# The half-empty low pass of the k, v and q products, written as two 64-row matmuls

## The chip, the cores and the metric

The kernel runs on one core of one Trainium2 chip. The time is device microseconds from launch to end of one execution; three executions of the kernel before took 755.6, 756.94 and 759.04 us, median 756.94. Beside the times there is one profiled execution with its trace.

## The reference

Two layers of linear attention alternate with two layers of a mixture of tiny experts, on x of 2048 x 576 in float32:

```python
def _A_ref(x, wqkv, wo):
    qkv = (x @ wqkv).reshape(B, S, 3, H, Dh)...      # 32 heads of 18
    phi = lambda t: jnp.where(t > 0, t + 1, jnp.exp(t)) + 1e-6
    pq, pk = phi(q), phi(k)
    kv = jnp.einsum("bhsd,bhse->bhde", pk, v)
    num = jnp.einsum("bhqd,bhde->bhqe", pq, kv)
    den = jnp.einsum("bhqd,bhd->bhq", pq, z)[..., None] + 1e-6
    return (num / den).reshape(B, S, D) @ wo
...
x = x + _A_ref(_layernorm(x, axis=-1), A_wqkv, A_wo)
x = x + _B_ref(_layernorm(x, axis=-1), B_w_q, B_k1, B_k2, B_u, B_v)
x = x + _A_ref(_layernorm(x, axis=-1), A_wqkv, A_wo)
x = x + _B_ref(_layernorm(x, axis=-1), B_w_q, B_k1, B_k2, B_u, B_v)
```

The change is in `x @ wqkv`, the products k, v and q of both attention layers.

## The kernel before

The 2048 tokens are 16 tiles of 128. For each tile and layer, `front_T` transposes the normalised x on TensorE (tile ptf) and splits the result in two: a high part, rounded by ScalarE to the matmul's number format (thif, line 102), and the low part that is left (tlof, by VectorE, line 103). The weights are split in the same way into whi and wlo. A product is then high x high + high x low + low x high, summed in PSUM.

The contraction runs over 576 rows, which are four blocks of 128 and one of 64 (block `rem`, number 2). So that block 2 fills the array too, its 64 rows stand twice in the transposed x, and its weights hold the high part in partitions 0 to 63 and the low part in 64 to 127 (`split_mixed`, lines 107 and 108). One pass over block 2 of thif then does high x high and high x low at once. The pass of tlof over block 2 does low x high in its upper 64 rows, and in its lower 64 rows low x low, which the other blocks leave out.

`passes` lists the 14 passes of a product: five of thif with whi, four of thif with wlo, five of tlof with whi. `product` (line 212) issues each pass as two matmuls, one for each part of the 576 columns, which go to two PSUM banks: 288 + 288 for k and q, 252 + 324 for v. That is 28 matmuls a product, and 96 products (16 tiles, two layers, k, v and q). Their results are ppk, ppv and ppq.

The order on each engine is that in which the code is written: `in_order` ties the instructions of TensorE, ScalarE, VectorE and GpSimd, stretch by stretch, to the order in which they were issued. That order is set by loops for the first tiles, by `step2` in the middle, and by long lists of pieces given to `play` in the other stretches. A DMA queue on SyncE brings weights and tiles in.

Other things on TensorE that the text speaks of: the `fold` matmuls (line 550) have 32 columns of stationary operand, and four of them go to four strips of 32 PSUM partitions; kva (lines 283 and 285) sums the attention state; ptf, ptb and pto are transposes (line 197). po (line 517) is the experts' output.

Of the kernel before, what the change touches and what calls it, by code (L numbers as in the profile page):

```python
# [12 lines left out]
F32R = mybir.dt.float32r  # L13
BF16 = mybir.dt.bfloat16
I32 = mybir.dt.int32
AF = mybir.ActivationFunctionType
# [5 lines left out]
S, D, H, DH = 2048, 576, 32, 18  # L22
P = 128
NT = S // P
DK, E, NE = 128, 8, 64
HC = 7 * DH
HALF = D // 2
# [11 lines left out]
def blocks(rem):  # L39

    rows, at = [], 0
    for b in range(NB):
        rows.append((at, b - (b > rem)))
        at += 64 if b == rem else P
    return rows


def passes(rem):
    rest = [b for b in range(NB) if b != rem]
    return ([("hi", b, "hi") for b in range(NB)] + [("hi", b, "lo") for b in rest]  # L50
            + [("lo", b, "hi") for b in range(NB)])
# [6 lines left out]
def network(ctx, tc, x_in, wqkv, wo, wq_t, k_t, u_t, v2, c_mask, c_mask4, c_ident, c_code, c_code1, c_scale, c_shift, out):  # L58
    nc = tc.nc

    cp = ctx.enter_context(tc.tile_pool(name="cp", bufs=1))
# [4 lines left out]
    def psum(name):  # L66
        return ps.tile([P, 1024], F32, tag="ps", name=name)
# [14 lines left out]

    whi = cp.tile([P, NB, 3 * D], F32R, name="whi")
    wlo = cp.tile([P, 4, 3 * D], F32R, name="wlo")
    ohi = cp.tile([P, NB, D], F32R, name="ohi")
    olo = cp.tile([P, NB, D], F32R, name="olo")
    shi = cp.tile([P, NB, 512], F32R, name="shi")
# [12 lines left out]
    def split(src, hi, lo, eng=nc.vector):  # L100

        nc.scalar.activation(hi, src, AF.Copy)  # L102
        eng.tensor_tensor(lo, src, hi.bitcast(F32), op=ALU.subtract)  # L103

    def split_mixed(src, dst):

        nc.scalar.activation(dst, src, AF.Copy)
        nc.vector.tensor_tensor(dst[64:], src[64:], dst[64:].bitcast(F32), op=ALU.subtract)
# [24 lines left out]
    def split_weight(tiles, c0, hi, lo, rem, which=range(NB), eng=nc.vector):  # L133
        for b in which:
            cols = slice(c0, c0 + D)
            if b != rem:
                split(tiles[b], hi[:, b, cols], lo[:, blocks(rem)[b][1], cols], eng)
            else:
                split_mixed(tiles[b], hi[:, b, cols])

    @contextmanager
    def in_order(*engines):
# [62 lines left out]
    def product(tt, hi, lo, cols, n, cut=HALF, rem=REM, by_block=False):  # L205

        o = psum(f"pp{n}")
        todo = sorted(passes(rem), key=lambda p: p[1]) if by_block else passes(rem)
        for i, (a, b, w) in enumerate(todo):
            wb = hi[:, b] if w == "hi" else lo[:, blocks(rem)[b][1]]  # L210
            for c0, c1, at in ((0, cut, 0), (cut, D, 512)):
                nc.tensor.matmul(o[:, at:at + c1 - c0], tt[a == "lo"][:, b, :], wb[:, cols + c0:cols + c1],  # L212
                                 start=(i == 0), stop=(i == len(todo) - 1))
        return o

    def phi(p, n):
# [7 lines left out]
    tt = {}  # L224
# [9 lines left out]
    def front_k(l, t):  # L234
        k = product(tt["f", l, t], whi, wlo, D, f"k{l}_{t}", by_block=(l == 0 and t == 0))
        yield
        tt["fk", l, t] = phi(k, f"k{l}_{t}")

    def front_v(l, t):
        v = product(tt["f", l, t], whi, wlo, 2 * D, f"v{l}_{t}", cut=2 * HC)  # L240
        yield
        vt = v5[t % 2]
        w = HC + 1
        for c, x in ((0, v[:, :2 * HC]), (2, v[:, 512:512 + 2 * HC])):
            nc.scalar.activation(vt[:, c * w:(c + 2) * w].rearrange("p (c e) -> p c e", c=2)[:, :, :HC],
                                 x.rearrange("p (c e) -> p c e", c=2), AF.Copy)
        yield
        nc.scalar.activation(vt[:, 4 * w:4 * w + 72], v[:, 512 + 2 * HC:512 + 2 * HC + 72], AF.Copy)

    def front_q(l, t):  # L250
        q = product(tt["f", l, t], whi, wlo, 0, f"q{l}_{t}")
        yield
        fq = phi(q, f"q{l}_{t}")
        nc.sync.dma_start(pq_d[l][t], fq)
# [438 lines left out]
    with in_order(*ALL):  # L693
        x0, x1 = xs.pop(("f", 0)), xs.pop(("f", 1))
        warm_up(14)
        rs0 = statistics(x0, "f0_0", soon=True)
        split_weight(wk_in, D, whi, wlo, REM, (0,))
        ys["f", 0, 0] = normalized(x0, rs0, "f0_0")
        split_weight(wk_in, D, whi, wlo, REM, (1, 2))
        run(0, (fT, 0, 1))  # L700
        warm_up(2)
        run(0, (fT, 0))
        split_weight(wk_in, D, whi, wlo, REM, (3,), nc.gpsimd)
        rs1 = statistics(x1, "f0_1", soon=True)
        split_weight(wk_in, D, whi, wlo, REM, (4,))
# [145 lines left out]
```

## Time and profile before

| | |
|---|---|
| median of three executions | 756.94 us |
| span of the profiled execution, first to last instruction | 753.7 us |
| matmuls | 5356 |
| VectorE busy | 456.8 us |
| ScalarE busy | 289.1 us |
| GpSimd busy | 197.7 us |
| DMA moved | 79.48 MB |

The profiled execution's span is the time from its first to its last instruction; the profile gives no further time for it, so what lies around the span is taken from the median, 3.2 us. In the rows, PE is TensorE's matmuls, PEld its weight loads, DVE VectorE, ACT ScalarE, POOL GpSimd. A timeline row gives start and length in us, engine, line, operation, the tile written and the tiles read, and how many instructions the row takes together. Where an engine was idle before, the bracket gives for how long and who released it. Line numbers are those of the kernel before.

### The profile page before, as it was taken

What the parts mean: (1) busy time and instruction counts of PE and PEld (TensorE: products, weight loads), DVE (VectorE), ACT (ScalarE), POOL (GpSimd) and SP (SyncE); (2) the same over time, 40 slices, a digit from 0 to 9 for tenths busy, and PEclk for the clock granted to TensorE, in tenths of its full rate; (3) what the DMA queues carried; (4) which work ended last, traced back from release to release, by engine and by line L of the source; (5) the groups of instructions that cost most, each with busy time, mean ns of one, the idle gap of its engine ahead of it and who ended that gap; (6) DMA issues with size and microseconds to landing.
All of it is one profiled execution on the core that took longest, in us unless ns stands there. A gap on an engine that the chain in (4) does not pass through costs nothing.

```text
span 753.7 us, 13987 instructions
## 1 busy us (share of the span) xinstructions
PE 736.8 (98%) x5356; PEld 693.2 (92%) x5356; DVE 456.8 (61%) x1008; ACT 289.1 (38%) x586; POOL 197.7 (26%) x540
## 2 busy tenths in 40 slices
PE   7999999999999999999999999999999999999996
PEld 5999989999998989999999999999999999999984
DVE  5532342324246887666666665563366789999996
ACT  5422232232333544444444443533234333343443
POOL 2110001000002543333333342230033343534331
PEclk9999999999999999999999999999999999999999
DMA  9736446631111322222232211321733213111201
GB/s 275 245 125 223 157 171 220 218 118 49 48 63 32 110 89 77 98 84 83 92 105 101 83 67 60 111 68 38 206 107 112 85 65 115 48 48 58 70 33 63
DMA packets 52267, 79.48 MB, mean 105 GB/s; under 512 B 5480, under 2 KB 22376, under 8 KB 52200
## 3 DMA queue, kind: packets, MB, share of 16 engines
q1 hardware_dynamic: 52200, 78.59, 31.8%
q8 instruction: 42, 0.69, 0.4%
q14 instruction: 25, 0.20, 0.1%
HBM read 55.01 MB, written 23.56 MB: 104 GB/s over the span
## 4 chain that ended last, share of the span: by engine, by line
PE 81%; DVE 10%; ACT 3%; issue 2%; POOL 2%; DMA 1%; SPq 0%; DVEq 0%; POOLq 0%; ACTq 0%
PE ppk L212 15%; PE ppv L212 15%; PE ppo L402 13%; PE pps L433 12%; PE ppq L212 11%; PE kva L283 4%; PE fold_ps L550 2%; PE ptf L197 2%; PE ptb L197 2%; PE po L517 2%; PE pto L197 2%; PE m L332 1%; DVE tloo L103 1%; DVE o L379 1%; DVE x L391 1%
## 5 line engine op out<-in xcount | busy, mean ns | idle before, releaser
L219 DVE TENSOR_SCALAR ek<-ek 128x576 f32<-128x576 f32 x32 | 14.7, 459 | 81.4 <-ACT ek L218 76.9
L212 PE MATMUL ppk<-whi,thif 128*128 128x288 f32 x320 | 50.4, 301 | 1.6 <-ACT thif L102 1.6
L402 PE MATMUL ppo<-ohi,thio 126*128 126x288 f32 (+1 forms) x320 | 50.9, 301 | 0.8 <-DVE ct L492 0.5
L212 PEld LDWEIGHTS ppk<-whi,thif 128*128 128x128 f32 x320 | 44.2, 188 | 5.6 <-issue 3.3
L163 POOL TENSOR_SCALAR rsf<-mvf 128x1 f32<-128x1 f32 x16 | 3.1, 192 | 175.6 <-DVE mvf L161 175.4
L212 PE MATMUL ppk<-whi,tlof 128*128 128x288 f32 x320 | 48.7, 296 | 0.3 <-DVE tlof L103 0.3
L212 PE MATMUL ppv<-whi,thif 128*128 128x252 f32 x320 | 48.0, 296 | 0.1
L187 ACT ACTIVATE yb<-x,rsb 128x640 f32<-128x640 f32 x32 | 29.5, 923 | 47.9 <-POOL rsb L180 47.9
L212 PE MATMUL ppv<-whi,tlof 128*128 128x252 f32 x320 | 47.6, 295 | 0.0
L219 DVE TENSOR_SCALAR eq<-eq 128x576 f32<-128x576 f32 x32 | 15.8, 493 | 51.7 <-ACT eq L218 51.7
L433 PE MATMUL pps<-shi,thib 128*128 128x512 f32 x160 | 44.4, 407 | 2.0 <-ACT thib L102 2.0
L402 PEld LDWEIGHTS ppo<-ohi,thio 126*128 126x128 f32 (+1 forms) x320 | 44.6, 189 | 1.9 <-issue 0.7
L212 PEld LDWEIGHTS ppk<-whi,tlof 128*128 128x128 f32 x320 | 44.6, 188 | 0.5 <-DVE tlof L103 0.5
L212 PEld LDWEIGHTS ppv<-whi,tlof 128*128 128x128 f32 x320 | 44.6, 188 | 0.0
L212 PEld LDWEIGHTS ppv<-whi,thif 128*128 128x128 f32 x320 | 44.2, 188 | 0.3 <-ACT thif L102 0.3
L438 ACT ACTIVATE s<-pps 128x512 f32<-128x512 f32 x32 | 19.1, 596 | 61.4 <-PE pps L433 61.4
L433 PE MATMUL pps<-shi,tlob 128*128 128x512 f32 x160 | 42.5, 395 | 0.0
L103 DVE TENSOR_TENSOR tlof<-ptf,thif 128x640 fp32r<-128x640 f32 x32 | 26.2, 818 | 24.3 <-ACT thif L102 24.2
L402 PE MATMUL ppo<-ohi,tloo 126*128 126x288 f32 x256 | 40.3, 295 | 0.0
L402 PE MATMUL ppo<-olo,thio 126*128 126x288 f32 x256 | 40.3, 296 | 0.0
L212 PE MATMUL ppk<-wlo,thif 128*128 128x288 f32 x256 | 39.9, 296 | 0.0
L212 PE MATMUL ppq<-whi 128*128 128x288 f32 x260 | 39.6, 299 | 0.1
(156 smaller groups left out, 1778.6 us busy)
## 6 DMA issues: line engine op xcount, KB each, us to landing
fold<-in_wq_t SPq DMA_DIRECT2D x64, 288.0 KB, 4.8
whi<-hl_d SPq DMA_DIRECT2D x26, 320.0 KB, 3.5
pq_d<-eq SPq DMA_DIRECT2D x19, 288.0 KB
pq<-pq_d SPq DMA_DIRECT2D x19, 288.0 KB, 3.3
xf<-in_x SPq DMA_DIRECT2D x16, 288.0 KB, 4.7
x<-in_x SPq DMA_DIRECT2D x16, 288.0 KB, 2.8
x_d<-x SPq DMA_DIRECT2D x16, 288.0 KB, 3.1
x<-x_d SPq DMA_DIRECT2D x16, 288.0 KB, 2.6
```

Source lines behind the costliest of these rows:

```text
L103: eng.tensor_tensor(lo, src, hi.bitcast(F32), op=ALU.subtract)
L187: nc.scalar.activation(y, x2, AF.Identity, scale=rs[:, 0:1], bias=rs[:, 1:2])
L197: nc.tensor.transpose(pt[:, b * P:(b + 1) * P], x, ident)
L212: nc.tensor.matmul(o[:, at:at + c1 - c0], tt[a == "lo"][:, b, :], wb[:, cols + c0:cols + c1], start=(i == 0), stop=(i == len(todo) - 1))
L219: nc.vector.tensor_scalar(e, e, 1.0, EPS, op0=ALU.min, op1=ALU.add)
L283: nc.tensor.matmul(a[:w, c * HC:(c + 1) * HC], vt[:, c * w:(c + 1) * w], fk[:, c * HC:(c + 1) * HC], start=(t == 0 and c == 0), stop=(t == ...
L332: nc.tensor.matmul(m[:c, h * 512:h * 512 + HALF], kvb[:n, b * HC:b * HC + c], wob[l][b][:n, h * HALF:(h + 1) * HALF], start=True, stop=True)
L402: nc.tensor.matmul(p[:, h * 512:h * 512 + HALF], hl[a][:r, b], w[:r, h * HALF:(h + 1) * HALF], start=(i == 0), stop=(i == len(todo) - 1))
L433: nc.tensor.matmul(p[:, :512], hl[a == "lo"][:, b, :], shi[:, b] if w == "hi" else slo[:, blocks(REM)[b][1]], start=(i == 0), stop=(i == l ...
L438: nc.scalar.activation(s[:, NE:], p[:, :512], AF.Copy)
L517: nc.tensor.matmul(p[:, b * 512:b * 512 + HALF], c[i], vmix[:, b * HALF:(b + 1) * HALF], start=(i == 0 and not based), stop=(i == 1))
L550: nc.tensor.matmul(p[32 * j:32 * j + 32, at:at + c1 - c0], kpad[:, ch // 2, 24 - 8 * a:56 - 8 * a], st[:, c0:c1], start=(a == 0), stop=(a ...
```

## The change

The pass of tlof over block 2 is taken out of the list of passes and written as two matmuls of 64 rows. The first takes rows 0 to 63 of the array (tlof's upper copy of the block with whi) for the first part of the columns. The second takes rows 64 to 127 (tlof's lower copy) for the other part of the columns, into the other PSUM bank. For the second one the high weights are needed in partitions 64 to 127, where whi holds low parts: they are put into a new tile wx, by one more ScalarE copy for each of k, v and q. What was low x low in that pass is no longer computed.

The pair stands last in k and q, and first in v. In the very first product of k, whose passes go block by block, the pair moves from the middle to the end.

```diff
+    wx = cp.tile([P, 2 * HALF + D - 2 * HC], F32R, name="wx")
...
             else:
+                cut, at = upper(c0)
+                nc.scalar.activation(wx[64:, at:at + D - cut], tiles[b][64:, cut:], AF.Copy)
                 split_mixed(tiles[b], hi[:, b, cols])
+
+    def upper(c0):
+
+        return {0: (HALF, 0), D: (HALF, HALF), 2 * D: (2 * HC, 2 * HALF)}[c0]
...
         todo = sorted(passes(rem), key=lambda p: p[1]) if by_block else passes(rem)
-        for i, (a, b, w) in enumerate(todo):
+        todo.remove(("lo", rem, "hi"))
+        todo = [None] + todo if cols == 2 * D else todo + [None]
+        for i, p in enumerate(todo):
+            flags = dict(start=(i == 0), stop=(i == len(todo) - 1))
+            if p is None:
+                at = upper(cols)[1]
+                nc.tensor.matmul(o[:, :cut], tt[1][:64, rem, :], hi[:64, rem, cols:cols + cut], **flags)
+                nc.tensor.matmul(o[:, 512:512 + D - cut], tt[1][64:, rem, :], wx[64:, at:at + D - cut], **flags)
+                continue
+            a, b, w = p
             wb = hi[:, b] if w == "hi" else lo[:, blocks(rem)[b][1]]
             for c0, c1, at in ((0, cut, 0), (cut, D, 512)):
-                nc.tensor.matmul(o[:, at:at + c1 - c0], tt[a == "lo"][:, b, :], wb[:, cols + c0:cols + c1],
-                                 start=(i == 0), stop=(i == len(todo) - 1))
+                nc.tensor.matmul(o[:, at:at + c1 - c0], tt[a == "lo"][:, b, :], wb[:, cols + c0:cols + c1], **flags)
```

The order on the engines, at three places. First TensorE at the border of k and v of tile 2, layer 0. A row gives the line, the operation, the tile written, the tiles read, partitions x columns of the output, and how many in a row. Before:

```order
L212 MATMUL ppk_2_556<-whi,thif_2_447 128x288 x10
L212 MATMUL ppk_2_556<-wlo,thif_2_447 128x288 x8
L212 MATMUL ppk_2_556<-whi,tlof_2_448 128x288 x10
L212 MATMUL ppv_2_589<-whi,thif_2_447 128x252
L212 MATMUL ppv_2_589<-whi,thif_2_447 128x324
```

With the change (lines 222 and 223 are the two 64-row matmuls, line 228 the others):

```order
L228 MATMUL ppk_2_560<-whi,thif_2_451 128x288 x10
L228 MATMUL ppk_2_560<-wlo,thif_2_451 128x288 x8
L228 MATMUL ppk_2_560<-whi,tlof_2_452 128x288 x8
L222 MATMUL ppk_2_560<-whi,tlof_2_452 128x288
L223 MATMUL ppk_2_560<-wx,tlof_2_452 128x288
L222 MATMUL ppv_2_593<-whi,tlof_2_452 128x252
L223 MATMUL ppv_2_593<-wx,tlof_2_452 128x324
L228 MATMUL ppv_2_593<-whi,thif_2_451 128x252
```

Of k's ten last matmuls two have become the pair, and v's pair follows directly; 26 of the products stand like this. Elsewhere a pair stands alone. The second place is TensorE at the first v of layer 1, behind the experts' output po. Before:

```order
L517 MATMUL po_1_3216<-vmix,thib_98_3178 128x288 x2
L517 MATMUL po_1_3216<-vmix,tlob_98_3179 128x288 x2
L212 MATMUL ppv_0_3227<-whi,thif_0_3203 128x252
L212 MATMUL ppv_0_3227<-whi,thif_0_3203 128x324
L212 MATMUL ppv_0_3227<-whi,thif_0_3203 128x252
```

With the change:

```order
L532 MATMUL po_1_3220<-vmix,thib_98_3182 128x288 x2
L532 MATMUL po_1_3220<-vmix,tlob_98_3183 128x288 x2
L222 MATMUL ppv_0_3231<-whi,tlof_0_3208 128x252
L223 MATMUL ppv_0_3231<-wx,tlof_0_3208 128x324
L228 MATMUL ppv_0_3231<-whi,thif_0_3207 128x252
L228 MATMUL ppv_0_3231<-whi,thif_0_3207 128x324
```

The first matmul of v read thif, and now reads tlof. The third place is ScalarE at the start, where the weights of k (wst_0 to wst_4, by block) are split. Before:

```order
L187 ACTIVATE yf_0_205<-xf_151,rsf_0_199 128x640
L102 ACTIVATE whi<-wst_1_157 128x576
L107 ACTIVATE whi<-wst_2_159 128x576
L102 ACTIVATE thif_0_217<-ptf_0_211 128x640
L102 ACTIVATE whi<-wst_3_162 128x576
```

With the change:

```order
L194 ACTIVATE yf_0_206<-xf_152,rsf_0_200 128x640
L103 ACTIVATE whi<-wst_1_158 128x576
L141 ACTIVATE wx<-wst_2_160 64x288
L108 ACTIVATE whi<-wst_2_160 128x576
L103 ACTIVATE thif_0_219<-ptf_0_213 128x640
L103 ACTIVATE whi<-wst_3_163 128x576
```

The copy into wx stands ahead of block 2's high part and of the first thif.

## The prediction, made before the changed kernel ran

> **What bounds the kernel now.** I read the page's busy times and slices first, then the windows by stage, then the starts of single matmuls in the timeline.
>
> ```profile
> PE 736.8 (98%) x5356; PEld 693.2 (92%) x5356; DVE 456.8 (61%) x1008; ACT 289.1 (38%) x586; POOL 197.7 (26%) x540
> PE   7999999999999999999999999999999999999996
> PEclk9999999999999999999999999999999999999999
> PE 81%; DVE 10%; ACT 3%; issue 2%; POOL 2%; DMA 1%; SPq 0%; DVEq 0%; POOLq 0%; ACTq 0%
> PE ppk L212 15%; PE ppv L212 15%; PE ppo L402 13%; PE pps L433 12%; PE ppq L212 11%; PE kva L283 4%; PE fold_ps L550 2%; PE ptf L197 2%; PE ptb L197 2%; PE po L517 2%; PE pto L197 2%; PE m L332 1%; DVE tloo L103 1%; DVE o L379 1%; DVE x L391 1%
> ```
>
> TensorE is busy in every slice but the first and the last, its clock is granted in full, and the chain that ends last runs through it for 81% of the span. The three products k, v and q alone (ppk, ppv, ppq) are 41% of the span on that chain (15, 15 and 11). But a matmul's end in this profile is modelled, and neighbours overlap, so "98% busy" can't tell a full engine from one with small gaps. Starts can.
>
> ```profile
> 29.73 1.23 PE L212 MATMUL ppq<-wlo,thif 128*128 128x288 f32 x8
> 30.80 1.50 PE L212 MATMUL ppq<-whi,tlof 128*128 128x288 f32 x10
> 32.14 1.04 PE L283 MATMUL kva<-ek,v 128*127 128x126 f32 x8
> ```
>
> Eight matmuls of 288 columns start between 29.73 and 30.80, ten between 30.80 and 32.14: 0.134 us each, although the page gives one some 0.295. The next group begins on the same beat, so here nothing waits and a product of 28 matmuls takes 28 beats.
>
> ```profile
> 40.00:175.00 135.00, 135.00 (x1168) 126.20 (x1167) 42.47 (x90) 39.39 (x95) 9.09 (x27) 1.00 0.51 174
> 300.00:480.00 180.00, 179.22 (x1287) 171.97 (x1287) 116.33 (x262) 79.55 (x163) 59.94 (x174) 1.00 0.26 87
> 620.00:680.00 60.00, 59.24 (x409) 55.95 (x409) 56.70 (x122) 22.80 (x44) 26.73 (x63) 1.00 0.20 66
> 720.00:753.70 33.70, 25.04 (x135) 20.43 (x133) 25.59 (x73) 12.90 (x27) 8.33 (x28) 0.95 0.14 53
> L212 PE MATMUL ppq<-whi x260: 288/294/514, 529.4 to 674.7; 128*128 128x288 f32 x130
> ```
>
> The columns after the stretch's length are PE, its weight loads, DVE, ACT and POOL. From 40 to 175 and from 300 to 480 us PE is full and no other engine passes 65%. Only from 620 on does DVE come level (56.70 of 60), and only after 720 does PE leave time free. The last product ends just after 674.7, so all 96 lie where PE sets the pace: a microsecond more or less on PE is one at the end.
>
> **What is saved.** In each of the 96 products (16 tiles, two layers, three products) one pass of two full matmuls becomes two of 64 rows, which can run together if the array takes both row halves at once. No matmul in this trace has 64 rows. The nearest are the fold matmuls, which use 32 of the array's columns each.
>
> ```profile
> 49.52 0.29 PE L285 MATMUL kva<-ek,v 128*73 128x72 f32 x2
> 49.58 0.23 PE L285 MATMUL kva<-ek,v 128*73 128x72 f32 x1
> 49.74 0.46 PE L550 MATMUL fold_ps<-fold,kpad 128*32 128x320 f32 x1
> 49.74 0.48 PE L550 MATMUL fold_ps<-fold,kpad 128*32 128x320 f32 x3
> 50.31 0.63 PE L550 MATMUL fold_ps<-fold,kpad 128*32 128x256 f32 x8
> 50.52 0.68 PE L550 MATMUL fold_ps<-fold,kpad 128*32 128x256 f32 x6
> 51.49 0.44 PE L550 MATMUL fold_ps<-fold,kpad 128*32 128x256 f32 x4
> 51.86 0.40 PE L212 MATMUL ppk<-whi,thif 128*128 128x288 f32 x1
> 52.09 0.43 PE L212 MATMUL ppk<-whi,thif 128*128 128x288 f32 x2
> ```
>
> One of 320 columns takes 0.46, three together 0.48; four of 256 take 0.44, and the next four start 0.21 after them (50.31, 50.52). So matmuls on separate strips do run side by side, each 0.01 to 0.02 behind the one before: I take 0.015. The bounds for a pair are 0.015 and a whole beat (no overlap).
>
> For k and q a pair then costs 0.134 + 0.015 instead of 0.268: 0.119 saved, 64 times, 7.6 us. In v the halves are of 252 and 324 columns:
>
> ```profile
> 298.92 0.43 PE L212 MATMUL ppv<-whi,tlof 128*128 128x252 f32 x2
> 299.04 0.43 PE L212 MATMUL ppv<-whi,tlof 128*128 128x324 f32 x2
> 299.19 0.42 PE L212 MATMUL ppv<-whi,tlof 128*128 128x252 f32 x2
> ```
>
> 252 columns take 0.12 (298.92 to 299.04), 324 take 0.15. Side by side they take 0.165 instead of 0.27: 0.10 saved, 32 times, 3.2 us. Together **10.8 us** saved.
>
> The Trainium skill, "TensorE: Matmul & The Clock Gate", section "Measured speedup vs the span model", lets each further tile of a pack add about 4 ns, less than this trace's 10 to 20. By it the saving would be 96 x 0.011 = 1.1 us larger; an estimate, and the trace decides.
>
> **What the switch costs.** The same rows show what going into tiles and out again costs. The 72-column kva matmuls follow each other after 0.06 (49.52, 49.58), so the fold could start at 49.64; it starts at 49.74: 0.10 lost. On the way out a next group would start 0.21 after 51.49, at 51.70; ppk starts at 51.86: 0.16 lost. And ppk's second matmul comes 0.23 after the first (52.09) instead of 0.134: another 0.10.
>
> The weight loads tell why: within a stream the load for the next matmul lies under the one that runs, but here it doesn't start before the array is empty.
>
> ```profile
> 51.31 0.14 PEld L550 LDWEIGHTS fold_ps<-fold,kpad 128*32 128x32 f32 x3
> 51.86 0.70 PEld L212 LDWEIGHTS ppk<-whi,thif 128*128 128x128 f32 x5 [0.41 <-issue]
> ```
>
> The load of ppk begins at 51.86, with its matmul, after 0.41 in which the loader waited for nothing that the profile shows. So a round trip costs **0.36 us** (0.10 + 0.16 + 0.10). All of it is between strips of columns and whole width; what it is between row halves and whole height no row shows. Bounds: 0, if halves of rows need no emptying; 0.46, if the entry also lays its load bare by 0.10, since a pair loads 128 columns and the fold 32. Below nothing I see no way: a switch removes no work. I take 0.36, the only whole round trip that the trace has.
>
> The Trainium skill, "TensorEngine Tiling (Array Packing)", section "Key Properties", says that changing the tiling mode, and not just the tile, drains TensorE. The fold's rows agree for columns (0.10 in, 0.16 out); for rows no run here shows it. By that rule the sum is the one below; without it, the one of the first rival.
>
> How often? In the new order of TensorE's instructions the 64-row pairs stand in 70 stretches: 26 times k's last pair directly ahead of v's first, and 44 times a pair alone (32 q, 6 k, 6 v). Before and after each stand full-height matmuls or transposes. 70 x 0.36 = **25.2 us**.
>
> **The smaller parts.** Three copies on ACT fill wx. The nearest row is 128x252 at 0.376:
>
> ```profile
> L245 ACT ACTIVATE v<-ppv x64: 362/376/438, 23.4 to 530.0; 128x252 f32<-128x252 f32 x64
> 8.22 0.69 ACT whi L107
> 8.94 0.76 DVE whi L108
> 9.72 0.83 DVE tlof L103
> 10.60 3.65 PE ppk L212 x24
> ```
>
> The last four rows are the chain of waits at the start. The first copy stands right ahead of that L107, so whi, tlof and the first product come about 0.4 later. The copies for v and q lie under running products. So +0.4 (bounds 0 and 1.2, all three bare).
>
> v now begins with its low part, so it waits for tlof, where it waited for thif. In the 26 v behind a k that tlof is already in use. Of the six v alone, two begin as soon as thif is there:
>
> ```profile
> 279.81 0.82 DVE L103 TENSOR_TENSOR tlof<-ptf,thif 128x640 fp32r<-128x640 f32 x1 [0.68 <-ACT thif L102]
> 279.83 1.36 PEld L212 LDWEIGHTS ppv<-whi,thif 128*128 128x128 f32 x10 [0.35 <-ACT thif L102]
> 513.88 0.83 DVE L103 TENSOR_TENSOR tlof<-ptf,thif 128x640 fp32r<-128x640 f32 x1 [0.52 <-ACT thif L102]
> 513.92 1.58 PE L212 MATMUL ppv<-whi,thif 128*128 128x252 f32 x10
> ```
>
> tlof ends 0.8 later each time, and behind v's first pair stands the rest of PE's queue. 2 x 0.8 = +1.6 (bounds 0, if the empty time also covers the switch and later slack takes the rest, and 1.6). Of the other four the tightest has its tlof 2.5 us early (468.85 + 0.82 against 472.18):
>
> ```profile
> 468.85 0.82 DVE L103 TENSOR_TENSOR tlof<-ptf,thif 128x640 fp32r<-128x640 f32 x1 [2.07 <-ACT thif L102]
> 472.18 0.36 PE L212 MATMUL ppv<-whi,thif 128*128 128x252 f32 x1
> ```
>
> **Sum.** 753.7 (span) - 10.8 + 25.2 + 0.4 + 1.6 = 770.1. The median of the runs shown is 756.94, 3.2 above the profiled span, which I add: **773.3 us**, 2.2% slower. No slack takes up the difference, since PE is the engine that is full; what DVE and ACT do moves back with it.
>
> **Rivals.**
> 1. *No price for row halves* (faster). The pairs overlap and the loads are drawn ahead as in any stream. For it: not every change of form empties the array.
>
> ```profile
> 301.95 0.29 PE L285 MATMUL kva<-ek,v 128*73 128x72 f32 x2
> 302.07 0.71 PE L197 MATMUL pto<-ident,o 128*128 128x128 f32 x5
> ```
>
> The transposes start 0.12 after two matmuls of 0.06, with nothing lost between 73 columns and full width. Against it: the fold's switch above, 0.36. 753.7 - 10.8 + 2.0 + 3.2 = 748.1; at best, with pairs wholly hidden (64 x 0.134 + 32 x 0.12 = 12.4) and the small parts covered, 744.5. DVE at 95% from 620 to 680 may take back up to 2 us of what the q products there save. The point of decision is 8.8 us over 70 stretches: below 0.126 per round trip the change gains, above it loses. The Trainium skill, "TensorEngine Tiling (Array Packing)", section "Theoretical Speedup", gives up to twice the speed where a dimension is at most 64; no row here shows that for rows, and by it alone this rival would be the outcome.
> 2. *Drain without bare loads.* Only the emptying is paid, 0.10 at each end: 70 x 0.20 = 14.0, so +5.2 and 762.1.
> 3. *The change doesn't do what it says*: the two halves run one after the other, with no switch price. Nothing saved, 2.0 added: 758.9. The fold's overlap speaks against it, though that is over columns.
> 4. *One after the other, and the switch is paid*: 25.2 + 2.0 on top, 784.1.
>
> **Chances.** Forecast 0.56 (its own range 771 to 780: price 0.36 with the small parts hidden, or 0.46 in full), first rival 0.20, second 0.10, third 0.10, fourth 0.04. Faster by over 0.5% (about 3.8 us, which is what a measurement of this kernel can tell from no change) is the first rival: 0.20. Within 0.5%: the third, 0.10. Slower: 0.70. To leave out no more than 2 in 10 the range has to reach into the first rival: 746 to 781 leaves out the fourth and the edges of the first and of the forecast.
>
> **What would show it.** In the profile after: a 64-row pair should start within 0.02 of each other (else 3 or 4). Between the last full matmul and the pair, and between the pair and the next full one, starts should be some 0.1 further apart than a beat, with the weight load beginning together with its matmul; the second matmul behind each switch should come at 0.23. If starts keep the 0.134 beat throughout, the first rival has it. The small parts show as ppk's first start at 9.9 instead of 9.55, and as waits on tlof ahead of two v of the second layer. The forecast is wrong above all if row halves switch without emptying the array.

## The result, and the profile after

The changed kernel took 770.17 us (median of four executions, 769.15 to 770.22), the kernel before 757.91 beside it (four executions, 755.60 to 759.04). The ratio is 1.0168, with a 95% interval of 1.0149 to 1.0188: 1.7% slower. The forecast was 773.3, 2.2% slower, in a range of 746 to 781. The profiled execution's span went from 753.7 to 768.3 us.

The page after, in the parts shown of before:

```profile
PE 748.7 (97%) x5356; PEld 683.0 (89%) x5356; DVE 457.8 (60%) x1008; ACT 292.1 (38%) x589; POOL 196.1 (26%) x540
PE   7999999999999999999999999999999999999996
PEclk9999999999999999999999999999999999999998
PE 81%; DVE 10%; ACT 3%; DMA 2%; issue 2%; POOL 1%; SPq 0%; DVEq 0%; POOLq 0%; ACTq 0%
```

At this height hardly anything has moved: as many matmuls, PE at 97%, the same engine on the chain. Only the weight loads tell something: busy for 683.0 us where it was 693.2, in a span that is 15 us longer. The starts of single matmuls show what happened. This is the timeline of TensorE at the border of k and v of a tile in layer 0, matmuls first, then the weight loads in the same stretch:

```profile
58.13 0.42 PE L228 MATMUL ppk<-whi,tlof 128*128 128x288 f32 x2
58.48 0.40 PE L222 MATMUL ppk<-whi,tlof 64*128 64x288 f32 x1
58.48 0.40 PE L223 MATMUL ppk<-wx,tlof 64*128 64x288 f32 x1
58.72 0.28 PE L222 MATMUL ppv<-whi,tlof 64*128 64x252 f32 x1
58.73 0.31 PE L223 MATMUL ppv<-wx,tlof 64*128 64x324 f32 x1
58.96 0.65 PE L228 MATMUL ppv<-whi,thif 128*128 128x252 f32 x3
59.18 0.42 PE L228 MATMUL ppv<-whi,thif 128*128 128x324 f32 x2
```

```profile
58.13 0.19 PEld L228 LDWEIGHTS ppk<-whi,tlof 128*128 128x128 f32 x1
58.48 0.18 PEld L222 LDWEIGHTS ppk<-whi,tlof 64*128 64x128 f32 x1 [0.16 <-issue]
58.48 0.18 PEld L223 LDWEIGHTS ppk<-wx,tlof 64*128 64x128 f32 x1
58.59 0.19 PEld L222 LDWEIGHTS ppv<-whi,tlof 64*128 64x128 f32 x1
58.59 0.19 PEld L223 LDWEIGHTS ppv<-wx,tlof 64*128 64x128 f32 x1
58.96 0.56 PEld L228 LDWEIGHTS ppv<-whi,thif 128*128 128x128 f32 x4 [0.18 <-issue]
```

The reader is to see four things. The two halves of a pair start together (58.48 and 58.48, 58.72 and 58.73). The first row takes two full matmuls together; the second of them started at 58.26, so the pair was due a beat later, at 58.39. It comes 0.09 late, and its weight load begins with it. The second pair is 0.24 behind the first, 0.10 more than a beat of 0.134: the first pair's load lay bare, that is, no running matmul covered it. And the way out repeats both: 58.96 is 0.23 behind 58.73 where 324 columns take 0.15, so 0.08 to 0.09 is lost, and the next matmul follows after 0.22 where 252 columns take 0.12, another 0.10. A round trip costs some 0.38 us, in four parts of about 0.1.

Ahead of transposes it is a little less. The same view at a lone q:

```profile
210.94 0.69 PE L228 MATMUL ppq<-whi,tlof 128*128 128x288 f32 x4
211.56 0.40 PE L222 MATMUL ppq<-whi,tlof 64*128 64x288 f32 x1
211.57 0.40 PE L223 MATMUL ppq<-wx,tlof 64*128 64x288 f32 x1
211.90 0.33 PE L204 MATMUL ptf<-ident,yf 128*128 128x128 f32 x1
212.06 0.49 PE L204 MATMUL ptf<-ident,yf 128*128 128x128 f32 x3
```

The first transpose comes 0.33 behind the pair, so 0.20 over a beat; the second 0.16 behind the first, 0.05 over the 0.11 of a transpose. With 0.09 on the way in that is 0.34. All 70 stretches have these intervals to within a few hundredths, apart from the two in which v waits for tlof.

### The profile page after: what moved, and what is told of

Its sections match the earlier page's. It is cut to its first block, busy times and chain, and to the rows that moved or that the text cites. A ratio compares the mean times of both kernels' runs of the same rounds, so it can differ in the third digit from the quotient of the medians.

```text
span 768.3 us, 13986 instructions
## 1 busy us (share of the span) xinstructions
PE 748.7 (97%) x5356; PEld 683.0 (89%) x5356; DVE 457.8 (60%) x1008; ACT 292.1 (38%) x589; POOL 196.1 (26%) x540
## 4 chain that ended last, share of the span: by engine, by line
PE 81%; DVE 10%; ACT 3%; DMA 2%; issue 2%; POOL 1%; SPq 0%; DVEq 0%; POOLq 0%; ACTq 0%
PE ppv L228 13%; PE ppk L228 13%; PE ppo L417 13%; PE ppq L228 12%; PE pps L448 12%; PE kva L298 3%; PE fold_ps L565 2%; PE ptf L204 2%; PE ptb L204 2%; PE po L532 2%; PE pto L204 2%; DMA wst<-in_wqkv 2%; PE m L347 1%; PE ppk L222 1%; PE ppq L222 1%
## 5 line engine op out<-in xcount | busy, mean ns | idle before, releaser
L228 PE MATMUL ppv<-whi,thif 128*128 128x252 f32 x320 | 50.8, 304 | 0.0
L104 DVE TENSOR_TENSOR tlob<-ptb,thib 128x768 fp32r<-128x768 f32 (+2 forms) x37 | 31.2, 844 | 15.6 <-ACT thib L103 15.4
L260 ACT ACTIVATE v<-ppv 128x252 f32<-128x252 f32 x64 | 20.9, 379 | 51.3 <-PE ppv L228 51.3
L228 PE MATMUL ppk<-whi,tlof 128*128 128x288 f32 x256 | 39.6, 294 | 0.2 <-DVE tlof L104 0.2
L228 PE MATMUL ppv<-whi,tlof 128*128 128x252 f32 (+1 forms) x256 | 39.0, 294 | 0.0
L228 PE MATMUL ppv<-wlo,thif 128*128 128x252 f32 (+1 forms) x256 | 38.9, 293 | 0.0
```

## The experiments

The theory to be tested: each stretch of 64-row work costs 0.34 to 0.385 us for going in and out, and each pair in it saves 0.13 (k, q) or 0.11 (v). By the starts in the trace this is 26 x 0.38 + 23 x 0.34 + 21 x 0.385 = 25.8 of price, less 64 x 0.130 + 32 x 0.112 = 11.9 saved: +13.9. Against it stood A (the loss is in the small parts: copies, order, waits on tlof), B (the pairs save next to nothing and a stretch costs about 0.2), and two that speak to single runs, C and D. The kernel before took 756.96 beside the first four kernels and 756.78 beside the last two. Beside the changed kernel it had taken 757.91, so a difference between the changed kernel and one of these runs is uncertain by about 1 us.

**Pairs only where k's and v's stand together.**

```diff
-        todo.remove(("lo", rem, "hi"))
-        todo = [None] + todo if cols == 2 * D else todo + [None]
+        lone = {f"k0_{t}" for t in (0, 13)} | {f"v0_{t}" for t in (1, 13)}
+        lone |= {f"{x}1_{t}" for x in "kv" for t in (0, 10, 11, 14)}
+        if n[0] != "q" and n not in lone:
+            todo.remove(("lo", rem, "hi"))
+            todo = [None] + todo if cols == 2 * D else todo + [None]
```

> 64-row pairs only in the 26 places where k's last pair stands directly ahead of v's first; q and the lone k and v keep the full-height pass in its old place. Theory (each stretch of 64-row work costs about 0.385 us for going in and out, each pair in it saves about 0.12): 26 x (0.385 - 0.24) = +3.8 us, and up to 1 for the copies into wx: 761 to 763 beside 757.9 before and 770.2 with the change. Rival A (the loss is in the small parts: the copies, v's low part first, the first k): those stay but for two waits on tlof, about 768.

Measured: 760.03 us, ratio 1.0044 (1.0030 to 1.0059). That is +3.1 over before. The theory's 761 to 763 was counted from 757.9; on the 756.96 measured here its +3.8 to +4.8 is about 761 to 762, some 1 us too high. A's 768 is out. Taking away 44 of the 70 stretches, and the two waits on tlof with them, took away 10 us of the loss.

**Both matmuls on the same half of the rows.**

```diff
-                nc.tensor.matmul(o[:, 512:512 + D - cut], tt[1][64:, rem, :], wx[64:, at:at + D - cut], **flags)
+                nc.tensor.matmul(o[:, 512:512 + D - cut], tt[1][:64, rem, :], hi[:64, rem, cols + cut:cols + D], **flags)
```

> Both 64-row matmuls on rows 0 to 63, so they can't run side by side; same tiling mode, same number of stretches. Theory: the saving of the overlap (64 x 0.129 + 32 x 0.113 = 11.9 us) is lost and the price stays: about 782. Rival B (the pairs save next to nothing as they are, and the price of a stretch is about 0.2): as with the change, 770.

Measured: 780.07 us, ratio 1.0306 (1.0290 to 1.0321), 9.9 above the changed kernel. In its timeline the matmuls of a stretch come one by one:

```profile
59.41 0.40 PE L222 MATMUL ppk<-whi,tlof 64*128 64x288 f32 x1
59.65 0.31 PE L223 MATMUL ppk<-whi,tlof 64*128 64x288 f32 x1
59.79 0.28 PE L222 MATMUL ppv<-whi,tlof 64*128 64x252 f32 x1
59.92 0.30 PE L223 MATMUL ppv<-whi,tlof 64*128 64x324 f32 x1
60.15 0.38 PE L228 MATMUL ppv<-whi,thif 128*128 128x252 f32 x1
```

The four take 0.74 until the full height is back (59.41 to 60.15), in the changed kernel 0.48 (58.48 to 58.96). So the overlap is real and is worth its 0.12 to 0.13 per pair; B is out. Of the 12 expected 9.9 reached the end.

**v's pair last.**

```diff
-        todo = [None] + todo if cols == 2 * D else todo + [None]
+        todo = todo + [None]
```

> v's pair last, as in k and q: 96 stretches of one pair in place of 70, and no v waits for tlof. Theory: 26 more round trips at 0.385 = +10.0, two waits of 0.8 to 1 less: 778 to 779. Rival A: only the waits go, 768. Rival B (0.2 per stretch): +5.2 - 1.7, about 774.

Measured: 776.75 us, ratio 1.0266 (1.0251 to 1.0282), 6.6 above the changed kernel. A says less than the changed kernel and is out; B's 774 lies below every run (775.83 to 778.15). The theory's 778 to 779 is a little high. A part of that is known: it counted every new stretch at 0.385, and in 21 of them v's pair now stands ahead of transposes, where the price is 0.34.

**The order of the change without 64-row tiles.**

```diff
-        todo.remove(("lo", rem, "hi"))
-        todo = [None] + todo if cols == 2 * D else todo + [None]
+        low = ("lo", rem, "hi")
+        todo.remove(low)
+        todo = [low] + todo if cols == 2 * D else todo + [low]
```

> The order of the change and its copies into wx, but the low pass of block 2 as two full-height matmuls: no 64-row tile at all. Theory: only the small parts are left, 0.4 to 1.4 at the start and 1.7 of waits on tlof: 759.5 to 761. Rival A: 768 to 770. Rival B: 759.5 to 761, as the theory.

Measured: 757.63 us, ratio 1.0015 (1.0005 to 1.0025), so 1.1 us (0.4 to 1.9) for copies, order and waits together; the profiled spans, 753.7 and 754.7, say 1.0. A is out for good, and the theory's small parts were up to 2 us too large. The two waits of v on tlof are in this kernel's list of waits in full:

```profile
PE ppv L229 <- DVE tlof L104: 1.6, 2, 1.0
```

The columns are the total, how often, and the longest. 1.6 of waits alone is more than the 1.0 to 1.1 of everything together, although the start is later too. The two traces show where the difference went. This kernel issues TensorE's matmuls for the same tiles in the same places as the kernel before, so each start can be compared with its counterpart. Up to 40 us it loses 1.3, and at the two waits 1.7, which is 3.0 in all. The products give 1.9 of that back: they run in a little less time. One k and v of layer 1 before, then with the order alone:

```profile
401.62 1.49 PE L212 MATMUL ppk<-whi,thif 128*128 128x288 f32 x10
405.35 1.49 PE L212 MATMUL ppv<-whi,thif 128*128 128x252 f32 x10
409.06 0.60 PE L197 MATMUL ptb<-ident,yb 128*128 128x128 f32 x4
```

```profile
402.28 1.48 PE L229 MATMUL ppk<-whi,thif 128*128 128x288 f32 x10
405.98 0.42 PE L229 MATMUL ppv<-whi,tlof 128*128 128x252 f32 x2
409.67 0.60 PE L204 MATMUL ptb<-ident,yb 128*128 128x128 f32 x4
```

Before, k takes 3.73 and v 3.71; here 3.70 and 3.69. It is much the same in nearly every tile, and behind 40 us no other group of matmuls moves by 0.1 in total, apart from the two waits. Why 28 matmuls take less in the new order is not shown.

**The low pass of block 2 left out.**

```diff
-        todo = [None] + todo if cols == 2 * D else todo + [None]
```

> The low pass of block 2 is left out of all products (that part of the result is missing), the copies into wx stay. Shows what the 64-row stretches take in all. Theory, from the starts in the changed kernel's trace (0.67 us per stretch of two pairs, 0.48 to 0.53 per lone pair, and 1.7 of waits on tlof): 41 us less than with the change, 729, if PE's time still reaches the end in full. Rival C (with less on PE, VectorE binds from 620 us on): 733 to 740.

Measured: 740.17 us, ratio 0.9784 (0.9769 to 0.9799). The theory's 729 is out by 11 us, and the end came only to C's upper edge. Without the pass, PE has 64 x 0.268 + 32 x 0.27 = 25.8 us less to do than before, and only 16.6 of it is seen at the end. The lists of waits say where most of the rest went: the rows of TensorE's list add up to 12.7 us before and to 19.7 here, in waits for VectorE from 6.5 to 11.4 and for ScalarE from 6.2 to 8.0. First a line of the kernel before, then two of this one (total, how often, longest):

```profile
PE ptb L197 <- DVE cg L498: 3.1, 2, 2.3
```

```profile
PE ptb L204 <- DVE cg L512: 4.1, 5, 2.3
PE ppq L227 <- DVE ek L235: 1.1, 2, 0.8
```

Is it C's reason, VectorE from 620 us on? The windows by stage, before and here (after the length come PE, its loads and DVE):

```profile
620.00:720.00 100.00, 99.16 (x665) 92.61 (x665) 93.74 (x214) 39.77 (x77) 41.89 (x114) 1.00 0.20 64
```

```profile
620.00:720.00 100.00, 96.62 (x625) 88.31 (x624) 93.26 (x223) 40.91 (x80) 40.34 (x118) 1.00 0.16 51
```

VectorE is as busy there as it was before. And start by start against the kernel with the order alone, 9.3 of the 25.8 us are not gained, and only 2.5 of these lie behind 620 us: 1.4 lie ahead of 40, 1.2 between 40 and 300, 2.7 between 300 and 480, 1.5 between 480 and 620. So C's number fits and its reason covers at most about a quarter of the loss; the rest is short waits for other engines, spread over most of the span.

**72 rows in place of 64.**

```diff
-                nc.tensor.matmul(o[:, :cut], tt[1][:64, rem, :], hi[:64, rem, cols:cols + cut], **flags)
-                nc.tensor.matmul(o[:, 512:512 + D - cut], tt[1][64:, rem, :], wx[64:, at:at + D - cut], **flags)
+                nc.tensor.matmul(o[:, :cut], tt[1][:72, rem, :], hi[:72, rem, cols:cols + cut], **flags)
+                nc.tensor.matmul(o[:, 512:512 + D - cut], tt[1][:72, rem, :], hi[:72, rem, cols + cut:cols + D], **flags)
```

> The pair as two matmuls of 72 rows from row 0 on, at the same places (8 rows of low x low come with it). Theory (the price hangs on the tile of 64 rows, not on fewer rows): full beat, no switch, as with full-height passes in that order: 759.5 to 761. Rival D (any matmul that doesn't fill the array's height empties it): 780 and more, since nothing overlaps either.

Measured: 758.2 us, ratio 1.0020 (1.0010 to 1.0029), near the order alone and 1.3 under the theory's range; D is out. The page's own lengths show the difference between the two kinds of matmul. First the 72 rows, then the 64 rows of the changed kernel (least, median and greatest length in ns of k's first matmul in the pair):

```profile
L222 PE MATMUL ppk<-whi,tlof x32: 295/295/298, 14.5 to 526.5; 72*128 72x288 f32 x32
```

```profile
L222 PE MATMUL ppk<-whi,tlof x32: 393/397/400, 15.1 to 536.1; 64*128 64x288 f32 x32
```

A matmul that uses 72 of the rows is as long as any other; with 64 rows, at the entry, it is 0.10 longer, and its weight load begins with it. The nearest kernel to compare with is the one with both matmuls on the same half: it differs from this one in 64 rows against 72 alone, and took 780.07 against 758.20. So rows left empty cost nothing at 72, and 64 rows cost the switch. Row counts between the two, and below 64, were not tried.

## Why the prediction was right

**What bounds the kernel.** The step "a microsecond more or less on PE is one at the end" held well upwards: 13.9 us more on PE and 1.1 of small parts make 15.0, and 12.3 came out between the medians, 14.6 between the spans. Against the kernel with the order alone, which has the same order of matmuls, 13.6 of the 13.9 are seen between the spans (754.7 to 768.3). It did not hold downwards: of 25.8 us less, 16.6 came out. The prediction had allowed for this only in its first rival, with up to 2 us for VectorE behind 620; the run with the pass left out lost 9, most of it ahead of 620. Had the switch been free, the 748 of that rival would probably not have been reached in full.

**What is saved.** Predicted 10.8, by the starts 11.9. The mechanism was right; the stagger inside a pair is 0.003 to 0.008 us (once 0.001), not the 0.015 taken from the fold's strips of columns. The Trainium skill's 4 ns per further tile ("TensorE: Matmul & The Clock Gate", section "Measured speedup vs the span model"), which the prediction set aside for the trace's 10 to 20, is about what row halves do here, 3 to 8 ns: 211.56 and 211.57 above differ by one step of the last printed digit. The run with both on the same half shows that the overlap reaches the end (9.9 us of it).

**What the switch costs.** Predicted 0.36 for each of 70 stretches, 25.2 in all; measured 0.34 to 0.385, 25.8 in all. The round trip of the fold, which is over columns, was the right row to go by, though its parts lay differently: the fold enters for 0.10 and leaves for 0.26, the pair pays 0.09 + 0.10 at each end. That 0.36 came so near was in part luck: the entry does lay its load bare, which the prediction had kept for its upper bound of 0.46, and the emptying on the way out is 0.09 where the fold has 0.16. The two nearly cancel. The drain that the Trainium skill states for a change of tiling mode ("TensorEngine Tiling (Array Packing)", section "Key Properties") is there for halves of rows too. This case's trace puts 0.09 us on it at each end, and 0.10 on the weight load that isn't drawn ahead. The count of 70 was right, and what each stretch does to the time is shown by the runs with 26 and with 96 of them: +3.1 and +19.8 us over before (760.03 and 776.75 against 756.96), beside +12.3 with 70. The run with 96 has the same 96 pairs as the changed kernel, so there the number of stretches alone was raised, apart from the two waits that went.

**The smaller parts.** Predicted 2.0, measured 1.1 (0.4 to 1.9) by the run with the order alone. The first product starts at 9.93, as the prediction said (9.9). Two rows of the changed kernel's timeline, the first k and the first v of layer 1:

```profile
9.93 0.54 PE L228 MATMUL ppk<-whi,thif 128*128 128x288 f32 x2 [1.75 <-ACT thif L103]
287.58 0.38 PE L222 MATMUL ppv<-whi,tlof 64*128 64x252 f32 x1 [0.98 <-DVE tlof L104]
```

The second row is one of the two waits on tlof, 1.6 us together, as predicted. Two things the prediction left out nearly cancel. The first product also waits inside, for low weights, which it didn't before:

```profile
PE ppk L228 <- DVE wlo L104: 0.8, 1, 0.8
```

In the kernel with the order alone the first product starts 0.5 later than before and ends 1.0 later (the next group comes at 15.05, before at 14.09); with 72 rows, and the same copies, it starts at 9.60 and ends 0.7 later. So 0.4 was too small for the start, and the start itself moves between profiles. Against that stand the 1.9 us by which the products run shorter in the new order. In that kernel it isn't later waits that give time back: outside the start, the two waits and the products, no group of matmuls moved by 0.1.

**The sum.** 770.1 was forecast for the span and 768.3 came. The saving was 1.1 too small, the price 0.6 too small and the small parts about 1 too large, which together is 1.5 of the 1.8. The 3.2 us for what lies around the span is a term of the wrong size: every execution on record with both figures is 1.7 to 1.9 longer than its span, such as 770.12 with 768.3. The rest of the 3.2 means that the profiled execution of before was a fast one. So 773.3 was 3.1 too high, 1.4 of it by this term, and the measured 770.17 lies just below the forecast's own 771 to 780.

**The rivals.** The first (no price for row halves) is refuted by the intervals above. The second (drain without bare loads) had half of the price: the loads are bare, 0.10 each. The third and fourth (one after the other) are refuted by the starts of the halves, at most 0.01 apart. What the fourth describes is what the run with both on the same half does: it took 780.07, where the fourth had 784.1.

No version of this change beat the kernel before. By the measured price a stretch must hold three pairs of 0.13 to break even; the best here with pairs, the 26 stretches of two, still cost 3.1 us. A stretch of three or more needs k, v and q open in PSUM at once, and was not tried.

## What to carry to other kernels

Using half of the array's rows twice pays only if enough such work stands together: here a round trip costs about 0.38 us, and a pair of 288 columns gives back 0.13, so by this sum it takes three pairs in a row to be even. Before such a change, count the stretches in the order of the instructions, not the matmuls, and look for any other switch of tiles in the trace to price it. And read gaps on TensorE from starts: the page's busy share said 98% before and 97% after, while 26 us of switching went in.

## What the hardware showed that was not expected

- Row halves are closer together than strips of columns: the two of a pair start 0.003 to 0.008 us apart, the fold's four mostly 0.013 (0.012 to 0.030).
- The price of a switch is about the same for both kinds of tile, 0.36 for strips of 32 columns and 0.34 to 0.385 for halves of 64 rows.
- With 64 rows in use a matmul in a full-height stream pays the switch, with 72 it doesn't: 780.07 us against 758.20, both with the two matmuls one after the other (397 ns long at the entry against 295).
- Leaving the low pass of block 2 out, work that fills TensorE for 25.8 us, gives 16.6 us. A TensorE that is full by its starts still stands close to other limits: most of the missing 9 us came back as short waits along most of the span.
- The order of the passes alone changes the length of a product: k took 3.70 us in place of 3.73, v 3.69 in place of 3.71. The cause is open.
